# Spreading the score groups over the first three columns of a gated attention and MoE kernel

## The chip, the cores and the metric

The kernel runs on one core of a Trainium2 chip. The metric is the device time of one execution, in microseconds. The engines are named as in the profile: PE (TensorE, matmuls; PEld is its weight load), DVE (VectorE), ACT (ScalarE), POOL (GpSimd) and SP (SyncE, which here only starts transfers). Each engine works through its own list of instructions in order and waits on semaphores for the others.

## What is computed

```python
def _attn_ref(u, v, z):                     # u, v: 8 x 3008 x 256, z: 8 x 3008 x 64
    scale = 1.0 / S
    scores = scale * np.matmul(z, z.transpose(0, 2, 1))
    attn = np.maximum(scores, 0.0) ** 2
    out = np.matmul(attn, v)
    return (u * out).astype(np.float32)

def _moe_ref(x, w_in, w_out):               # x: 24064 x 256, w_in: 256 x 2048
    h = x @ w_in
    g = h * np.cos(h)
    return (g @ w_out).astype(np.float32)
```

The output of the first, flattened to 24064 rows, is the input of the second.

## The kernel before, in words

**Columns and pieces.** A batch has 3008 positions: 24 blocks of 128 (the last is a half), or 6 columns of 512. For each column J the kernel makes the squared ReLU of the scores against all blocks, in pieces A of four blocks by one column, key (b, J, I) with I from 0 to 5. A *score group* (emit_score, L178) makes half a piece: two matmuls (L187) of 64 rows each, which run side by side in the two halves of the array, into a two-bank score buffer E; a ReLU from PSUM into an r tile, on ACT (L200) or, for the groups listed in on_dve (8, 15, 21, 28, 34), on DVE (L198); and a square on DVE into the piece (L204 or L207). The score matrix is symmetric, so from column 3 of the first batch on a piece that exists already is turned by a DMA transpose on SP (L234, or L228 inside a diagonal piece) in place of being computed again. Columns 0 to 2 of the first batch, which this case is about, compute all of their 12 groups. The list of groups is fixed; done_groups counts through it.

**Value matmuls.** emit_value (L248) multiplies one block of a piece with v. For each block k and each half dh of the 256 output columns there are two such matmuls, t = 0 and 1, again side by side in the two halves of the array; below, such two are a *pair*. The four sums of a column are in the banks M0, M1 (dh = 0) and in one E buffer (dh = 1). A column has 23 blocks by 2 halves, and the last half block split over both halves: 47 pairs.

**Buffers.** PSUM holds M0, M1 and three score buffers E0, E1, E2 of two banks. take_e hands out E buffers in turn (e_order). In the first three columns one E buffer holds the dh = 1 sums, so the score groups have two. There are three r tiles and 22 pieces.

**Start.** z of the first batch comes in six pieces of four blocks. DVE casts pieces 0 and 1, POOL casts 2 to 5 (L501), between which it issues the first v loads. PE turns each piece (turn_on_pe, L505: four transposes of 128 x 128) into PSUM, and ACT or DVE copies it to zT (copy_turned, L513 and L515). Pieces 2 to 5 are turned into one tile, turned4, that lies where E2 will be; each turn into it waits for the copy of the one before. Matmuls on a zero tile (filler, L534) stand between them.

**Columns 0 to 2** (phase_a_first, L334). For each I, the four dh = 0 pairs and then the four dh = 1 pairs of piece I are issued, then a burst of quota[I] score groups, then a transpose or other small work. Four groups are made ahead of column 0; each later group belongs to a piece that is read about two I later, and the last four of each column to the next column. In column 0, the turns and copies of pieces 4 and 5 (last_pieces) stand between the first four dh = 0 pairs and the first dh = 1 pairs, since the dh = 1 sums go to E2. At the end of a column, gate_sum adds the two banks of each half: a copy on ACT (L260), then an add on DVE (L261). The products with u (gate_mul, L276) come in the next column after I = 1, and uT, the turned u, comes by a DMA transpose (turn_u, L156). hold (L332) is a small copy on POOL that keeps the load of the next u behind the sums.

**Around them.** Between columns 1 and 2 stand four blocks of the hidden layer (emit_h: L385 matmuls, ACT cosine L393, DVE product L395), and w_out is loaded on POOL's queue ahead of them (L561). After column 2 the kernel goes into its steady form: phase_b (hidden layer and output matmuls, L385 and L407) and phase_a (a later column) by turns, to the end.

Of the kernel before, what the change touches and what calls it, by code (L numbers as in the profile page):

```python
# [14 lines left out]
def kernel(  # L15
# [74 lines left out]
    def drop_piece(key):  # L90
        i = pieces.pop(key)
        if pending.get(i):
            pending[i] = "dropped"
        else:
            free_pieces.append(i)
# [53 lines left out]
    def load_u(s):  # L149
        t = upool.tile([P, 4, D], FP16, name="u16")  # L150
        load_rows(t, u, s // NC, s % NC)
        u16s[s] = t

    def turn_u(s):
        t = upool.tile([P, 8, P], FP16, name="uT")
        nc.sync.dma_start_transpose(t, u16s.pop(s).rearrange("p j d -> p (j d)"))  # L156
        uTs[s] = t
# [17 lines left out]
    turn_slots = {}  # L175
    done_groups = [0]

    def emit_score(on_dve=False):  # L178
        b, J, I, h = groups[done_groups[0]]
        done_groups[0] += 1  # L180
        cut = I == J and not (b == 0 and J < 3)
        W = 2 * P if cut and h == 0 else width(J)
        zT = zTs[b]
        e = E[take_e()]
        for t in range(2):
            k = 4 * I + 2 * h + t
            nc.tensor.matmul(  # L187
                e[:, t, 0:W],
                zT[t * H:(t + 1) * H, k * P:(k + 1) * P],
                zT[t * H:(t + 1) * H, J * CW:J * CW + W],  # L190
                start=True,
                stop=True,
            )
        key = (b, J, I)
        a = new_piece(key) if h == 0 else piece(key)
        r = rpool.tile([P, 2, CW], FP16, name="r")
        if on_dve:
            nc.vector.tensor_scalar(r[:, :, 0:W], e[:, :, 0:W], 0.0, None, ALU.max)  # L198
        else:
            nc.scalar.activation(r[:, :, 0:W], e[:, :, 0:W], AF.Relu)  # L200
        if I > J:
            a4 = a.rearrange("p (k t j) -> p t k j", k=4, j=P)[:, 2 * h:2 * h + 2, :, :]
            r4 = r.rearrange("p t (k j) -> p t k j", j=P)
            nc.vector.tensor_tensor(a4, r4, r4, ALU.mult)  # L204
        else:
            a4 = a.rearrange("p (k w) -> p k w", w=CW)[:, 2 * h:2 * h + 2, 0:W]
            nc.vector.tensor_tensor(a4, r[:, :, 0:W], r[:, :, 0:W], ALU.mult)  # L207
        if h == 0:
            return
        if cut or (I > J and (b, J, I) not in direct):  # L210
            turns.append(((b, I), key))
            turns.sort(key=lambda t: t[0])
            turn_slots[key] = pieces[key]
            pending[pieces[key]] = "held"

    def emit_turns(due, more=0):
        while turns and (turns[0][0] <= due or more > 0):
            if turns[0][0] > due:
                more -= 1
            (b, c), key = turns.pop(0)  # L220
            b, J, I = key
            i = turn_slots[key]
            a = piece_bufs[i]
            if I == J:
                a4 = a.rearrange("p (k w) -> p k w", w=CW)
                for rr in range(2, 4):
                    rows = P if J * 4 + rr < NB - 1 else H
                    nc.sync.dma_start_transpose(  # L228
                        a4[:, 0:2, rr * P:rr * P + rows],
                        a[0:rows, rr * CW:rr * CW + 2 * P],  # L230
                    )
            else:
                d = new_piece((b, I, J))
                nc.sync.dma_start_transpose(d.rearrange("p (n j) -> p n j", j=P), a)  # L234
            if pending.pop(i) == "dropped":
                free_pieces.append(i)
# [10 lines left out]
    def emit_value(b, J, k, t, dh, bank, start, stop):  # L247
        nc.tensor.matmul(  # L248
            bank[:, 0:width(J)],
            vs[b, k // 4][t * H:(t + 1) * H, k % 4, dh * P:(dh + 1) * P],  # L250
            value_rhs(b, J, k, t),
            start=start,
            stop=stop,
        )

    def gate_sum(s, b0, b1):
        W = width(s % NC)
        s0 = spool.tile([P, CW], FP32, name="s0")
        s1 = spool.tile([P, CW], FP32, name="s1")
        nc.scalar.copy(s0[:, 0:W], b0[:, 0:W])  # L260
        nc.vector.tensor_tensor(s1[:, 0:W], b1[:, 0:W], s0[:, 0:W], ALU.add)  # L261
        return s1

    def gate_mul(s, dh, s1):
        J = s % NC
        b = s // NC
        W = width(J)
        if s not in xs:
            if J == NC - 1 and b % 2 == 1:
                xs[s] = xodd  # L270
            else:
                xs[s] = xpool.tile([P, 2, CW], FP16, name="x")
        x = xs[s]
        uT = uTs[s].rearrange("p (k d) j -> p k d j", d=2)
        nk = W // P
        nc.vector.tensor_tensor(  # L276
            x[:, dh, 0:nk * P].rearrange("p (k j) -> p k j", j=P),
            s1[:, 0:nk * P].rearrange("p (k j) -> p k j", j=P),
            uT[:, 0:nk, dh, :],
            ALU.mult,  # L280
        )
        if nk < 4:
            dst = x[:, dh, nk * P:W] if b % 2 == 1 else xodd[:, dh, W:CW]
            nc.vector.tensor_tensor(
                dst, s1[:, nk * P:W], uT[:, nk, dh, 0:W - nk * P], ALU.mult
            )
# [44 lines left out]
    def hold(src):  # L331
        nc.gpsimd.tensor_copy(mark[:, 0:1], src)  # L332

    def phase_a_first(s, on_dve, quota, before_dh1=None):  # L334
        b, J = s // NC, s % NC
        if before_dh1 is None:
            ea = e_order.pop(0)
            acc = [M, [E[ea][:, 0, :], E[ea][:, 1, :]]]
        else:
            acc = [M, None]  # L340
        last = NB - 1
        for I in range(NC):
            for dh in range(2):
                if acc[dh] is None:
                    before_dh1()
                    ea = e_order.pop()
                    acc[1] = [E[ea][:, 0, :], E[ea][:, 1, :]]
                for k in range(4 * I, min(4 * I + 4, last)):
                    for t in range(2):
                        emit_value(  # L350
                            b, J, k, t, dh, acc[dh][t], k == 0,
                            k == last - 1 and t != dh,
                        )
            if I == NC - 1:
                emit_value(b, J, last, 0, 0, acc[0][0], False, True)
                emit_value(b, J, last, 1, 1, acc[1][1], False, True)
            drop_piece((b, J, I))
            if I == NC - 1:
                if s == 0:
                    turn_u(0)  # L360
                late_sums.extend(gate_sum(s, *acc[dh]) for dh in range(2))
                hold(late_sums[0][0:1, 0:1])
                load_u(s + 1)
            for _ in range(quota[I]):
                emit_score(on_dve=done_groups[0] in on_dve)
            if s > 0:
                emit_turns((0, 0), 1)
                if I == 0:
                    turn_u(s)
                if I == 1:  # L370
                    for dh in range(2):
                        gate_mul(s - 1, dh, late_sums.pop(0))
        e_order.append(ea)

    def mwidth(m):
# [134 lines left out]
    def copy_turned(g):  # L510
        dst = zTs[0][:, g * CW:(g + 1) * CW]
        if g == 0:
            nc.scalar.copy(dst, turned[g])  # L513
        else:
            nc.vector.tensor_copy(dst, turned[g])  # L515
# [16 lines left out]
    def filler(n):  # L532
        for i in range(n):
            nc.tensor.matmul(M[i % 2], warm[:, 0:P], warm, start=True, stop=True)  # L534

    on_dve = (8, 15, 21, 28, 34)
    emit_score()
    emit_score()
    filler(2)
    for g in range(2, 4):  # L540
        turn_on_pe(g)
        copy_turned(g)
        filler(1)
        emit_score()

    def last_pieces():
        for g in range(4, NC):
            turn_on_pe(g)
            copy_turned(g)
        E.append(ppool.tile([P, 2, CW], FP32, name="E2", tag="E2"))  # L550
        e_order.append(2)

    for g in range(2, NC):
        load_v(0, g)
    load_u(0)
    nc.gpsimd.dma_start(w_in16, moe_w_in.rearrange("(k p) f -> p k f", p=P))

    halves = [(0, NB // 2), (NB // 2, NB)]
    phase_a_first(0, on_dve, (2, 2, 2, 2, 2, 2), last_pieces)
    phase_a_first(1, on_dve, (3, 3, 2, 2, 2, 0))  # L560
    nc.gpsimd.dma_start(w_out16, moe_w_out.rearrange("(k p) f -> p k f", p=P))  # L561
    for i in range(4):
        emit_h(0, i)
    phase_a_first(2, on_dve, (3, 3, 3, 3, 2, 0))
    assert done_groups[0] == need[3]
    for dh in range(2):
        gate_mul(2, dh, late_sums.pop(0))
# [59 lines left out]
```

## Time and profile before

| | us |
|---|---|
| median of 9 runs | 1241.62 |
| lowest and highest | 1240.0, 1243.92 |
| the profiled execution | 1243.92 |
| its span in the profile | 1242.1 |
| PE busy | 1223.0 |
| DVE busy | 810.1 |
| ACT busy | 806.1 |

The profile shows one execution. A busy share of an engine is the time in which an instruction of it was under way; a matmul's end is modelled. A window row gives its start and end, its length, then busy time and (instructions) of PE, PEld, DVE, ACT and POOL, then the granted share of PE's full clock, the mean busy share of the DMA engines, and GB/s. A row of the chain gives start, duration, engine, written tile, line and count. "issue" in the chain is time in which the engine waited for nothing that the profile shows.

The first instructions of the start, from the timeline (start, duration, engine, line, what; in brackets the idle time before and what ended it):

```profile
4.91 0.60 POOL L501 CAST z<-z 128x512 f16<-128x512 f32 x1 [3.60 <-DMA z<-in_z_dram]
5.07 0.60 PE L187 MATMUL E<-zT 64*128 64x512 f16 x4 [0.29 <-ACT zT L513]
5.50 2.86 ACT L200 ACTIVATE r<-E 128x1024 f16<-128x1024 f32 x3 [0.49 <-PE E L187]
6.56 2.36 DVE L207 TENSOR_TENSOR A<-r 128x1024 f16<-128x1024 f16 x2 [1.31 <-ACT r L200]
7.67 1.72 POOL L501 CAST z<-z 128x512 f16<-128x512 f32 x2
8.85 0.41 DVE L515 COPY zT<-turned 128x512 f16<-128x512 f16 x1
9.31 0.38 PE L505 MATMUL turned<-id,z 128*128 128x128 f16 x4 [2.33 <-DVE zT L515]
10.07 1.31 PE L248 MATMUL M<-A,v 64*128 64x512 f16 x8
12.43 0.58 PE L505 MATMUL turned<-id,z 128*128 128x128 f16 x4 [0.52 <-DVE zT L515]
13.53 1.04 PE L248 MATMUL E<-A,v 64*128 64x512 f16 x4 [0.52 <-DVE zT L515]
```

The copy of piece 2 stands in DVE's list behind the first two squares (6.56 to 8.92), and the turn of piece 3 on PE waits for it.

### The profile page before, as it was taken

Reading aid. Unit: us, or ns where it says so; the run is one execution under the profiler, and the core shown is the slowest. Engines: PE = TensorE matmul, PEld = TensorE weight load, DVE = VectorE, ACT = ScalarE, POOL = GpSimd, SP = SyncE. Lnnn points to the kernel's source line nnn. Section 1 sums busy time; section 2 is a strip of 40 time slices with the busy share of each in tenths; the row PEclk is TensorE's granted clock in tenths of the full one; section 3 lists DMA queues with packets and bytes.
Section 4 is the critical chain, followed back from the end, with each engine's and each line's share of the span. In section 5 each row is a group of like instructions: output and inputs, shape, how many; then the busy total and the mean of one; then the engine's idle time right before and its main releaser. Section 6 shows DMA issues by size and latency. Waiting matters only on the chain.

```text
span 1242.1 us, 23270 instructions
## 1 busy us (share of the span) xinstructions
PE 1223.0 (98%) x9775; PEld 696.0 (56%) x9775; DVE 810.1 (65%) x947; ACT 806.1 (65%) x918; POOL 132.2 (11%) x185
## 2 busy tenths in 40 slices
PE   8799999999999999999999999999999999999998
PEld 3355655556555555555555555655555555555565
DVE  5866766666666666666666666666666666666555
ACT  5666667666666666666666676666766666666445
POOL 3030211003000030000300003000121001000000
PEclk8999999999999999999999999999999999999999
DMA  9999797649976499844998359972597726953201
GB/s 144 157 159 157 100 173 130 118 90 120 149 118 120 81 117 160 139 87 98 143 143 134 69 98 153 163 120 69 104 173 125 133 60 110 162 102 69 46 18 51
DMA packets 467161, 144.80 MB, mean 117 GB/s; under 512 B 391536, under 2 KB 466800, under 8 KB 467056
## 3 DMA queue, kind: packets, MB, share of 16 engines
q1 hardware_dynamic: 368304, 110.11, 50.1%
q0 software_dynamic: 97216, 32.78, 26.9%
q8 instruction: 76, 1.25, 0.4%
q10 hardware_dynamic: 1536, 0.43, 0.2%
q14 instruction: 29, 0.24, 0.1%
HBM read 66.32 MB, written 24.64 MB: 73 GB/s over the span
## 4 chain that ended last, share of the span: by engine, by line
PE 96%; DVE 2%; ACT 1%; issue 1%; ACTq 0%; DVEq 0%
PE M L407 26%; PE E L385 26%; PE M L248 20%; PE E L248 19%; PE E L187 5%; ACT r L200 1%; DVE g L395 0%; DVE r L198 0%; DVE A L207 0%; DVE s L261 0%; PE E L520 0%; ACT c L393 0%; DVE A L204 0%; PE E L407 0%; DVE zT L515 0%
## 5 line engine op out<-in xcount | busy, mean ns | idle before, releaser
L395 DVE SCALAR_TENSOR_TENSOR g<-E,c 128x1024 f16<-128x1024 f32 (+1 forms) x384 | 456.7, 1201 | 219.7 <-ACT c L393 218.4
L393 ACT ACTIVATE c<-E 128x1024 f16<-128x1024 f32 (+1 forms) x384 | 381.1, 1006 | 182.0 <-PE E L385 181.6
L200 ACT ACTIVATE r<-E 128x1024 f16<-128x1024 f32 (+1 forms) x337 | 323.5, 965 | 132.1 <-PE E L187 125.2
L407 PE MATMUL M<-w_out,g 128*128 128x256 f16 x2992 | 373.7, 273 | 1.1 <-DVE g L395 0.6
L248 PEld LDWEIGHTS <-v 64*128 64x128 f16 x4512 | 218.7, 94 | 262.9 <-issue 24.9
L385 PE MATMUL E<-x,w_in 128*128 128x512 f16 (+1 forms) x1408 | 347.6, 375 | 0.6 <-DVE s L261 0.3
L407 PEld LDWEIGHTS <-g 128*128 128x128 f16 x3008 | 294.2, 98 | 94.0 <-DVE g L395 0.9
L248 PE MATMUL M<-A,v 64*128 64x512 f16 (+1 forms) x2256 | 282.8, 374 | 0.6 <-DVE s L261 0.5
L248 PE MATMUL E<-A,v 64*128 64x512 f16 (+1 forms) x2256 | 277.0, 373 | 0.5 <-DVE zT L515 0.5
L204 DVE TENSOR_TENSOR A<-r 128x1024 f16<-128x1024 f16 x240 | 165.5, 692 | 109.6 <-ACT r L200 108.5
L385 PEld LDWEIGHTS <-w_in 128*128 128x128 f16 x1536 | 146.4, 98 | 126.3 <-issue 21.0
L187 PE MATMUL E<-zT 64*128 64x512 f16 (+2 forms) x684 | 123.5, 363 | 8.4 <-DVE r L198 4.1
L426 ACT ACTIVATE o<-M 128x512 f32<-128x512 f32 x94 | 50.2, 585 | 63.4 <-PE M L407 63.4
L207 DVE TENSOR_TENSOR A<-r 128x512 f16<-128x512 f16 (+1 forms) x102 | 58.7, 577 | 46.5 <-ACT r L200 45.5
L136 POOL DMA_DIRECT2D u<-in_u_dram x48 | 36.8, 771 | 454.8 <-DMA uT<-u 454.4
L136 POOL DMA_DIRECT2D v<-in_v_dram x48 | 35.9, 754 | 403.9 <-PE E L187 341.0
L187 PEld LDWEIGHTS <-zT 64*128 64x128 f16 x684 | 34.7, 94 | 51.0 <-issue 13.1
L276 DVE TENSOR_TENSOR x<-s,uT 128x512 f16<-128x512 f32 (+1 forms) x88 | 59.5, 679 | 2.8
L261 DVE TENSOR_TENSOR s<-E,s 128x512 f32<-128x512 f32 (+1 forms) x48 | 32.6, 680 | 34.8 <-ACT s L260 34.8
L260 ACT COPY s<-E 128x512 f32<-128x512 f32 (+1 forms) x48 | 27.8, 579 | 39.7 <-PE E L248 39.7
L261 DVE TENSOR_TENSOR s<-M,s 128x512 f32<-128x512 f32 (+1 forms) x48 | 32.4, 675 | 6.0 <-ACT s L260 6.0
L260 ACT COPY s<-M 128x512 f32<-128x512 f32 (+1 forms) x48 | 27.5, 573 | 8.2 <-PE M L248 7.8
(33 smaller groups left out, 125.4 us busy)
## 6 DMA issues: line engine op xcount, KB each, us to landing
out_dram<-o SPq DMA_DIRECT2D x87, 256.0 KB, 2.7
v<-in_v_dram POOLq DMA_DIRECT2D x40, 256.0 KB, 6.7
u<-in_u_dram POOLq DMA_DIRECT2D x40, 256.0 KB, 9.4
z<-in_z_dram POOLq DMA_DIRECT2D x14, 368.0 KB, 15.6
A<-A SPq DMA_TRANSPOSE x207, 4.4
v<-in_v_dram POOLq DMA_DIRECT2D x8, 192.0 KB, 11.1
u<-in_u_dram POOLq DMA_DIRECT2D x8, 192.0 KB, 4.1
out_dram<-o SPq DMA_DIRECT2D x10, 128.0 KB, 2.8
```

The costliest lines, as they stand in the source:

```text
L136: nc.gpsimd.dma_start(t[:, 0:full, :], src[b, g * CW:g * CW + full * P, :].rearrange("(j p) d -> p j d", p=P),)
L187: nc.tensor.matmul(e[:, t, 0:W], zT[t * H:(t + 1) * H, k * P:(k + 1) * P], zT[t * H:(t + 1) * H, J * CW:J * CW + W], start=True, stop=True,)
L200: nc.scalar.activation(r[:, :, 0:W], e[:, :, 0:W], AF.Relu)
L204: nc.vector.tensor_tensor(a4, r4, r4, ALU.mult)
L207: nc.vector.tensor_tensor(a4, r[:, :, 0:W], r[:, :, 0:W], ALU.mult)
L248: nc.tensor.matmul(bank[:, 0:width(J)], vs[b, k // 4][t * H:(t + 1) * H, k % 4, dh * P:(dh + 1) * P], value_rhs(b, J, k, t), start=start, ...
L261: nc.vector.tensor_tensor(s1[:, 0:W], b1[:, 0:W], s0[:, 0:W], ALU.add)
L276: nc.vector.tensor_tensor(x[:, dh, 0:nk * P].rearrange("p (k j) -> p k j", j=P), s1[:, 0:nk * P].rearrange("p (k j) -> p k j", j=P), uT[:, ...
L385: nc.tensor.matmul(e[:, f, 0:W], w_in16[:, k, ft * P:(ft + 1) * P], x[:, k, 0:W], start=(k == 0), stop=(k == 1),)
L393: nc.scalar.activation(c[:, :, 0:W], e[:, :, 0:W], AF.Sin, bias=half_pi, scale=inv_s2)
L395: nc.vector.scalar_tensor_tensor(g[:, :, 0:W], e[:, :, 0:W], 1.0, c[:, :, 0:W], ALU.mult, ALU.mult)
L407: nc.tensor.matmul(y_bank(m, k), gs[m, ft // 2][:, ft % 2, k * P:(k + 1) * P], w_out16[:, ft, :], start=(ft == 0 and (k % 2 == 0 or (final ...
```

## The change

In the columns, the steps of a column (47 pairs) are listed first, and n score groups are placed singly after given steps: with n = 12 after steps 2, 5, 9, 12, 16, 20, 23, 27, 31, 34, 38, 42, with n = 14 after 2, 5, 8, 11, 14, 17, 20, 23, 26, 29, 32, 35, 38, 42. The number of groups a column, their order and the on_dve list are as before. The sums of a column now follow its last pair with no score group in between. A piece is dropped, a transpose and turn_u or the gate multiplies are issued, right after the last pair of an I.

At the start, piece 2 is turned and copied ahead of the first score group. A square can be held back (later), and the squares of the first four groups are put behind copies: DVE's list is now copy 2, copy 3, square 0, square 1, copy 4, square 2, copy 5, square 3. All six pieces are turned before the first value matmul, two of the four filler matmuls are gone, and column 0 takes its E2 buffer at its beginning like the other columns. The lists on POOL and SP keep their order.

```diff
-    def emit_score(on_dve=False):
+    def emit_score(on_dve=False, later=None):
...
+        def square():
+            if I > J:
+                a4 = a.rearrange("p (k t j) -> p t k j", k=4, j=P)[:, 2 * h:2 * h + 2, :, :]
+                r4 = r.rearrange("p t (k j) -> p t k j", j=P)
+                nc.vector.tensor_tensor(a4, r4, r4, ALU.mult)
...
+        if later is None:
+            square()
         else:
-            a4 = a.rearrange("p (k w) -> p k w", w=CW)[:, 2 * h:2 * h + 2, 0:W]
-            nc.vector.tensor_tensor(a4, r[:, :, 0:W], r[:, :, 0:W], ALU.mult)
+            later.append(square)
...
-    def phase_a_first(s, on_dve, quota, before_dh1=None):
+    def phase_a_first(s, n):
         b, J = s // NC, s % NC
...
+        ea = e_order.pop(0)
+        acc = [M, [E[ea][:, 0, :], E[ea][:, 1, :]]]
         last = NB - 1
...
+        steps = [
+            (dh, k)
+            for I in range(NC)
+            for dh in range(2)
+            for k in range(4 * I, min(4 * I + 4, last))
+        ] + [(2, last)]
+        lo, hi = 2, 42
+        at = {}
+        for i in range(n):
+            p = lo + (hi - lo) * i // (n - 1)
+            at[p] = at.get(p, 0) + 1
+        for i, (dh, k) in enumerate(steps):
+            if dh == 2:
                 emit_value(b, J, last, 0, 0, acc[0][0], False, True)
                 emit_value(b, J, last, 1, 1, acc[1][1], False, True)
...
+            else:
+                for t in range(2):
+                    emit_value(
+                        b, J, k, t, dh, acc[dh][t], k == 0, k == last - 1 and t != dh
+                    )
+            if dh > 0 and (k % 4 == 3):
+                drop_piece((b, J, k // 4))
+                if s > 0:
+                    emit_turns((0, 0), 1)
+                    if k < 4:
+                        turn_u(s)
+                    elif k < 8:
+                        for d in range(2):
+                            gate_mul(s - 1, d, late_sums.pop(0))
+            for _ in range(at.get(i, 0)):
                 emit_score(on_dve=done_groups[0] in on_dve)
...
+        if s == 0:
+            turn_u(0)
+        late_sums.extend(gate_sum(s, *acc[dh]) for dh in range(2))
+        hold(late_sums[0][0:1, 0:1])
+        load_u(s + 1)
         e_order.append(ea)
...
+    squares = []
+    turn_on_pe(2)
+    copy_turned(2)
+    emit_score(later=squares)
+    emit_score(later=squares)
+    turn_on_pe(3)
+    filler(1)
+    copy_turned(3)
+    squares.pop(0)()
+    emit_score(later=squares)
+    squares.pop(0)()
+    turn_on_pe(4)
+    filler(1)
+    copy_turned(4)
+    emit_score(later=squares)
+    squares.pop(0)()
+    turn_on_pe(5)
+    copy_turned(5)
+    squares.pop(0)()
+    E.append(ppool.tile([P, 2, CW], FP32, name="E2", tag="E2"))
+    e_order.insert(0, 2)
...
-    phase_a_first(0, on_dve, (2, 2, 2, 2, 2, 2), last_pieces)
-    phase_a_first(1, on_dve, (3, 3, 2, 2, 2, 0))
+    phase_a_first(0, 12)
+    phase_a_first(1, 12)
...
-    phase_a_first(2, on_dve, (3, 3, 3, 3, 2, 0))
+    phase_a_first(2, 14)
```

More of the change, by code (lines that the diff above doesn't have):

```diff
@@ L200, in emit_score @@
             nc.scalar.activation(r[:, :, 0:W], e[:, :, 0:W], AF.Relu)
[L201 to L204, printed above, removed]
-        else:
-            a4 = a.rearrange("p (k w) -> p k w", w=CW)[:, 2 * h:2 * h + 2, 0:W]
-            nc.vector.tensor_tensor(a4, r[:, :, 0:W], r[:, :, 0:W], ALU.mult)
+        def square():
[4 more added lines that the diff above has]
+            else:
+                a4 = a.rearrange("p (k w) -> p k w", w=CW)[:, 2 * h:2 * h + 2, 0:W]
+                nc.vector.tensor_tensor(a4, r[:, :, 0:W], r[:, :, 0:W], ALU.mult)
+        if later is None:
+            square()
+        else:
+            later.append(square)
         if h == 0:
@@ L332, in hold @@
         nc.gpsimd.tensor_copy(mark[:, 0:1], src)
-    def phase_a_first(s, on_dve, quota, before_dh1=None):
+    def phase_a_first(s, n):
         b, J = s // NC, s % NC
[L336 to L340, printed above, removed]
-        last = NB - 1
[L342 to L354, printed above, removed]
+        ea = e_order.pop(0)
+        acc = [M, [E[ea][:, 0, :], E[ea][:, 1, :]]]
+        last = NB - 1
+        steps = [
[11 more added lines that the diff above has]
+            if dh == 2:
@@ L355, in phase_a_first @@
                 emit_value(b, J, last, 0, 0, acc[0][0], False, True)
                 emit_value(b, J, last, 1, 1, acc[1][1], False, True)
[L357 to L364, printed above, removed]
-                emit_score(on_dve=done_groups[0] in on_dve)
@@ L366, in phase_a_first @@
[L366 to L372, printed above, removed]
+            else:
+                for t in range(2):
[11 more added lines that the diff above has]
+                            gate_mul(s - 1, d, late_sums.pop(0))
@@ L536 @@
     on_dve = (8, 15, 21, 28, 34)
[L537 to L551, printed above, removed]
+    squares = []
[19 more added lines that the diff above has]
+    e_order.insert(0, 2)
     for g in range(2, NC):
```

## The prediction

> **What bounds the kernel now.** I read the page first, for where TensorE is not full:
>
> ```profile
> span 1242.1 us, 23270 instructions
> ...
> PE   8799999999999999999999999999999999999998
> ...
> PEclk8999999999999999999999999999999999999999
> ...
> PE 96%; DVE 2%; ACT 1%; issue 1%; ACTq 0%; DVEq 0%
> ```
>
> TensorE is the bound (96% of the chain that ended last), and only the first two or three of the 40 slices have room. Then the windows, cut at the stages: start, column 0, column 1, the four blocks of hidden layer (emit_h), column 2, first output stage, rest.
>
> ```profile
> core 0: us, PE busy (x) PEld busy (x) DVE busy (x) ACT busy (x) POOL busy (x), PEclk, DMA share, GB/s
> 0.00:10.07 10.07, 6.26 (x36) 2.52 (x37) 5.02 (x9) 5.04 (x6) 5.86 (x13) 1.00 0.72 113
> 10.07:28.40 18.33, 17.13 (x129) 7.96 (x126) 9.55 (x15) 10.44 (x12) 4.81 (x8) 0.81 1.21 182
> 28.40:45.50 17.10, 13.79 (x118) 6.33 (x116) 13.45 (x20) 11.55 (x13) 0.96 (x2) 1.00 0.65 114
> 45.50:50.00 4.50, 3.94 (x20) 1.50 (x20) 4.27 (x6) 4.15 (x6) 2.07 (x3) 1.00 1.03 162
> 50.00:70.90 20.90, 15.70 (x124) 7.08 (x124) 14.18 (x20) 12.04 (x13) 0.00 (x0) 0.92 1.07 157
> 85.50:1242.00 1156.50, 1151.98 (x9263) 661.26 (x9262) 753.25 (x870) 753.71 (x860) 109.74 (x148) 1.00 0.75 114
> ```
>
> After 85.5 us TensorE idles 4.5 us in 1156, so whatever column 2 gains is carried to the end. In the columns the clock is granted at 0.81 and 0.92, and busy time (which contains modelled ends) falls short of the span. Last the chain in order of time, in column 2:
>
> ```profile
> 55.67 0.23 PE E L187 x2
> ...
> 56.84 1.94 ACT r L200 x2
> ...
> 59.41 1.29 DVE x L276 x2
> 60.70 1.15 DVE r L198
> ...
> 62.29 1.71 PE M L248 x8
> 64.00 1.57 PE E L248 x8
> ```
>
> A burst of three score groups has two score buffers; the third waits for a ReLU (ACT L200, or DVE L198 behind two gate multiplies L276). The value matmuls after it then stand at 1.71 us for eight, where the chain elsewhere has 0.86: half clock.
>
> **The price of one step.** Eight value matmuls are four pairs: 0.86 / 4 = 0.215 us a pair. Four score matmuls are two groups in 0.43: 0.215 a group. A column is 47 pairs. With 12 groups it is 59 x 0.215 = 12.7 us, with 14 it is 61 x 0.215 = 13.1. Before, columns 0 to 2 and the hidden blocks took 60.8 us (10.07 to 70.9).
>
> **The score's latency,** from the timeline: group at t, ReLU 0.43 later (5.07 to 5.50), 1.02 long, square 0.03 later, 0.69 long: the square ends at t + 2.2. Queued ReLUs follow 0.92 apart (two in 1.94), queued squares 0.61. In the new order groups are 4 or 5 steps apart (3 or 4 pairs and themselves): 0.86 to 1.08 us. With two buffers a group may start when the ReLU two before it is over, t + 1.5 against 1.7 to 2.2: no wait on ACT. A DVE ReLU (1.22) is another matter, below. Pieces are due late enough: groups 4 and 5 stand at steps 2 and 5, their piece is read at step 16, 11 pairs and 3 groups or 3.0 us later, against 2.2.
>
> **Start.** Piece 2's cast ends at 5.51 (POOL 4.91 + 0.60); its turn now precedes the first score group, which slips from 5.07 to about 5.8. DVE copies pieces 2 and 3 by about 7.75 (cast 3 ends 6.99, four turns, copy 0.42). Then squares 0 and 1: 2.36 us for two beside POOL's casts, less where those are over (9.39): done about 9.8. Copy 4 ends 10.2, piece 5 is turned by 10.5, and the first value matmul stands at 10.5 (10.07 before). The v piece it needs was there at 10.07; the second, issued at 6.92 with a median landing of 5.5, is there at 12.4, its first use at 10.5 + 8 pairs + 2 groups = 12.65. Square 2 and copy 5 end at 11.3, so the fifth pair, into E2, stands at 11.6, where it stood at 13.53. If the squares take 1.2 us to the end, all of this is 0.7 later.
>
> **Column 0.** 12.7 us, plus the DVE ReLU of group 8: square 7 ends 1.12 after group 8 starts, the ReLU at 2.34; group 10, which needs the buffer, is due after 9 steps, 1.94. Wait 0.45. Ends at 10.5 + 13.15 = 23.65.
>
> **Column 0 to 1.** Before, two groups stood behind the sums as cover. Now none does, and group 15 (DVE ReLU) stands at step 42. From its start: square 14 ends at 1.12, ReLU 2.34, square 15 at 3.0, the sum that frees bank M1 at 3.7 (add 0.68). The column ends at 5 steps, 1.08. TensorE waits 2.6 us; before, 0.5 with work in front. Next at 26.25.
>
> **Column 1.** 12.7, plus group 21: its ReLU is queued behind two gate multiplies (1.29) and square 20. From group 20: square 19 ends at 1.1, multiplies 2.35, square 20 at 3.0, ReLU 4.25; group 23 is due after 14 steps, 3.0. Wait 1.25. Ends at 40.2.
>
> **Hidden blocks.** Unchanged, bound by DVE: 45.54 to 49.98, 4.45 us. To 44.65.
>
> **Column 2.** 13.1, plus 1.1 for its first groups, which wait for DVE to empty E0 and E1 (0.32 + 0.74 before; the groups come earlier now, so there is no less), plus group 34 behind the multiplies. From group 32: square 32 ends at 2.2, multiplies 3.45, square 33 at 4.1, ReLU 5.35; group 36 is due after 16 steps, 3.45. Wait 1.9. Ends at 60.75. The handover to the output stage is as before.
>
> **Transfers.** The order on SP and POOL is the same; w_out is issued after column 1's sums. Its 14.9 us from 48.17 end 15.9 after that sum (46.46 + 0.68 = 47.14); in the new walk the sum ends near 41.6, w_out lands at 57.5, and is read near 61.9. Cover 4.4 us. u, turned beside it in 10.3, ends no later.
>
> **Sum.** 70.9 - 60.75 = 10.1 us gained, half clock not counted. For that:
>
> ```profile
> 7.27:10.68 3.41, 1.37 (x13) 0.69 (x14) 3.00 (x5) 1.50 (x3) 3.41 (x5) 1.00 1.10 123
> 31.16:34.57 3.41, 2.05 (x18) 0.99 (x19) 2.29 (x4) 2.52 (x3) 0.00 (x0) 1.00 0.57 71
> 58.47:61.88 3.41, 1.07 (x10) 0.43 (x7) 3.15 (x6) 1.33 (x2) 0.00 (x0) 1.00 1.76 173
> 61.88:65.30 3.42, 3.41 (x18) 1.54 (x19) 1.62 (x3) 0.60 (x1) 0.00 (x0) 0.50 0.96 211
> ```
>
> The clock fell after stretches of 3.41 us in which TensorE was busy 40% and 31%, and did not after one of 60%. A full stretch at half clock costs 1.7. In the new walk three stretches can come near 40%: the start, the 2.6 us wait, the 1.9 us wait; it hangs on how the stretches lie. Bounds: no fall, 0; three, 5.1. I take 1.0, nearer the first, since each wait fills a stretch only if it lies wholly inside.
>
> [...]
>
> Gain 9.1. The profiled execution took 1243.92, its span 1242.1 and 1.8 around it: 1243.92 - 9.1 = **1234.8**. It is the longest of the nine runs, 2.3 over their median; as its two clock falls (3.4) are already taken out, I subtract no more.
>
> **Rivals.**
> - *Waits and clock take half back (0.12).* All three waits drop the clock: 1234.8 + 4.1 = 1238.9. For: DVE is already the fullest of the small engines (13.45 of 17.1 in column 1). Against: full columns restore the clock in one stretch.
> - *Start only (0.05).* Even spacing gives nothing because the DVE ReLUs set the pace: 20.9 and 17.1 stay, column 0 ends at 26.25 with its wait in place of 29.14 (M1's restart): 1243.92 - 2.9 = 1241. For: waits of 1.25 and 1.9 remain. Against: of the waits before score groups, 3.6 us in four are on ACT, in the third group of a burst, and there are no bursts left.
> - *w_out becomes the bound (0.06): slower.* The stage shrinks by 10 us but the transfer doesn't; transposes share it. TensorE waits at the first output matmul once w_out lands after 61.9, and the kernel is slower once it lands after 61.9 + 9.1 = 71, 28.6 us from issue, where 14.9 was seen. At 30 us: 1245.3. Against: twice the measured time.
>
> **How the numbers follow.** Forecast 0.77, its own range 1231.5 (no fall, and the 2.3 to the median taken off) to 1237.5 (a second and third fall in part). To 1239 with the first rival. About 0.2% (2.5 us) can be told from no change: faster is below 1239.1, forecast and nearly all of the first rival, 0.88; same 0.06; slower 0.06.
>
> **What would show it.** Right: first E2 value matmul near 11.6; score groups alone between pairs; waits before L187 only behind DVE ReLUs; a bare wait of 2.6 at column 0's end; column 2 ending near 61 to 62. Wrong: ReLU waits at every group, half clock over a whole column, or PE waiting for w_out.

## The result, and the profile after

| | before | changed |
|---|---|---|
| median, us | 1240.8 (32 runs) | 1235.34 (10 runs) |
| lowest and highest | 1239.8, 1243.92 | 1233.56, 1238.14 |
| the profiled execution | 1243.92 | 1235.34 |
| its span | 1242.1 | 1233.6 |

The ratio of the changed kernel to the one before is 0.9955, 95% interval 0.9948 to 0.9963: 5.5 us less by the medians (8.5 between the two profiled spans; why the two differ is shown below). The median of before is that of all 32 runs, 0.8 under the nine known at the prediction.

The windows of the changed kernel, cut at the same stages as those of before (start, column 0, column 1, the four hidden blocks, column 2, and the rest after the first output stage):

```profile
core 0: us, PE busy (x) PEld busy (x) DVE busy (x) ACT busy (x) POOL busy (x), PEclk, DMA share, GB/s
0.00:10.44 10.44, 7.76 (x41) 3.41 (x42) 5.01 (x10) 5.95 (x7) 6.36 (x14) 1.00 0.71 112
10.44:23.75 13.31, 13.26 (x120) 6.11 (x119) 9.98 (x16) 9.91 (x10) 4.24 (x7) 1.00 1.19 179
23.75:41.70 17.95, 15.02 (x118) 7.15 (x117) 12.64 (x18) 11.82 (x13) 0.96 (x2) 0.90 0.93 160
41.70:46.16 4.46, 3.91 (x18) 1.47 (x17) 4.12 (x5) 4.14 (x6) 2.07 (x3) 1.00 1.08 190
46.16:62.40 16.24, 13.92 (x124) 6.89 (x124) 14.22 (x20) 11.92 (x13) 0.00 (x0) 1.00 1.30 189
77.10:1233.40 1156.30, 1151.79 (x9262) 661.19 (x9258) 753.25 (x870) 753.55 (x860) 110.82 (x150) 1.00 0.76 115
```

Column 0 went from 18.33 us to 13.31 and column 2 from 20.90 to 16.24. Column 1, with the wait before it, stands at 17.95: its clock is 0.90, and the wait at column 0's end (23.75 to 26.11) lies in it. The rest takes 1156.30 us against 1156.50: what the columns gained was carried to the end.

What TensorE waited for from 10 us to the end of column 2 (what waited and for what: us in total, times, longest):

```profile
PE E L187 <- DVE r L198: 2.6, 2, 1.6
PE M L254 <- DVE s L267: 1.3, 1, 1.3
PE turned L513 <- DVE zT L523: 1.0, 1, 1.0
PE M L254 <- ACT s L266: 0.7, 1, 0.7
```

Before, the first lines of the same view (10 to 72 us) were:

```profile
PE E L187 <- DVE r L198: 4.1, 4, 2.3
PE E L187 <- ACT r L200: 3.6, 4, 0.9
```

The waits on ACT's ReLUs are gone; two waits on DVE's are left. What stands in front of them on DVE, in column 2 of the changed kernel (timeline; L205 square, L282 gate multiply, L198 ReLU):

```profile
53.05 0.69 DVE L205 TENSOR_TENSOR A<-r 128x1024 f16<-128x1024 f16 x1 [0.22 <-ACT r L200]
53.66 1.29 DVE L282 TENSOR_TENSOR x<-s,uT 128x512 f16<-128x512 f32 x2
54.86 0.68 DVE L205 TENSOR_TENSOR A<-r 128x1024 f16<-128x1024 f16 x1
55.46 1.22 DVE L198 TENSOR_SCALAR r<-E 128x1024 f16<-128x1024 f32 x1
```

And TensorE at the same place and at column 0's end:

```profile
54.26 0.83 PE L254 MATMUL M<-A,v 64*128 64x512 f16 x6
56.73 0.28 PE L187 MATMUL E<-zT 64*128 64x256 f16 x2 [1.65 <-DVE r L198]
```

```profile
23.35 0.38 PE L254 MATMUL M<-A,v 64*128 64x512 f16 x1
23.37 0.38 PE L254 MATMUL E<-A,v 64*128 64x512 f16 x1
24.40 0.37 PE L254 MATMUL M<-A,v 64*128 64x512 f16 x1 [0.65 <-ACT s L266]
26.11 0.80 PE L254 MATMUL M<-A,v 64*128 64x512 f16 x5 [1.33 <-DVE s L267]
26.55 0.57 PE L187 MATMUL E<-zT 64*128 64x512 f16 x2
26.77 0.57 PE L254 MATMUL M<-A,v 64*128 64x512 f16 x2
26.99 1.21 PE L254 MATMUL E<-A,v 64*128 64x512 f16 x4
```

One score group fell due at 54.9 (three pairs after 54.26) and ran at 56.73, when DVE's ReLU (55.46 + 1.22) was over. At column 0's end TensorE has one matmul between 23.6 and 26.11, and soon after that the four E matmuls take 1.21 us where 0.6 is usual: the clock has fallen, granted at 0.50 from 27.21 to 30.63 us.

### The profile page after: what moved, and what is told of

Read it like the earlier page. It is cut to its first block, busy times and chain, and to the rows that moved or that the text cites. A ratio compares the mean times of both kernels' runs of the same rounds, so it can differ in the third digit from the quotient of the medians.

```text
span 1233.6 us, 23267 instructions
## 1 busy us (share of the span) xinstructions
PE 1220.0 (99%) x9773; PEld 695.6 (56%) x9773; DVE 809.5 (66%) x947; ACT 806.6 (65%) x918; POOL 132.1 (11%) x185
## 3 DMA queue, kind: packets, MB, share of 16 engines
q8 instruction: 76, 1.25, 0.4%
## 4 chain that ended last, share of the span: by engine, by line
PE 96%; DVE 2%; ACT 1%; issue 1%; DMA 0%; POOL 0%; SPq 0%; ACTq 0%
PE M L415 26%; PE E L393 26%; PE M L254 19%; PE E L254 18%; PE E L187 5%; ACT r L200 1%; DVE g L403 0%; DVE r L198 0%; DVE A L208 0%; DMA z<-in_z_dram 0%; DVE s L267 0%; DVE A L205 0%; DVE x L282 0%; ACT c L401 0%; PE E L415 0%
## 5 line engine op out<-in xcount | busy, mean ns | idle before, releaser
L205 DVE TENSOR_TENSOR A<-r 128x1024 f16<-128x1024 f16 x240 | 165.4, 691 | 104.8 <-ACT r L200 103.8
L187 PE MATMUL E<-zT 64*128 64x512 f16 (+2 forms) x684 | 127.5, 364 | 3.5 <-DVE r L198 2.6
L282 DVE TENSOR_TENSOR x<-s,uT 128x512 f16<-128x512 f32 (+1 forms) x88 | 59.5, 679 | 2.8
## 6 DMA issues: line engine op xcount, KB each, us to landing
z<-in_z_dram POOLq DMA_DIRECT2D x14, 368.0 KB, 15.6
```

Of the source, the lines that this page charges most:

```text
L187: nc.tensor.matmul(e[:, t, 0:W], zT[t * H:(t + 1) * H, k * P:(k + 1) * P], zT[t * H:(t + 1) * H, J * CW:J * CW + W], start=True, stop=True,)
L282: nc.vector.tensor_tensor(x[:, dh, 0:nk * P].rearrange("p (k j) -> p k j", j=P), s1[:, 0:nk * P].rearrange("p (k j) -> p k j", j=P), uT[:, ...
```

## The experiments

Each ratio compares a run with runs of before on the same chip. The experiments ran in three sets, each on a chip of its own; the medians of before were 1241.47 (the two parts alone, none on DVE, 8 and 28 on DVE), 1240.25 (the two with zero-tile matmuls, the kernel before with none on DVE, u ahead) and 1241.46 (the new start with none on DVE, u further back). Where medians of different sets are subtracted below, the difference by the ratios stands beside it.

### The two parts alone

The new start with the old bursts (against the changed kernel; phase_a_first itself is that of before):

```diff
...
-    phase_a_first(0, 12)
+    phase_a_first(0, on_dve, (2, 2, 2, 2, 2, 2))
-    phase_a_first(1, 12)
+    phase_a_first(1, on_dve, (3, 3, 2, 2, 2, 0))
-    phase_a_first(2, 14)
+    phase_a_first(2, on_dve, (3, 3, 3, 3, 2, 0))
```

> The new start (turns and copies ahead of the squares) with the old bursts of two and three groups. Theory (the two parts gain separately): the first E2 pair moves from 13.53 to about 11.5, 1.9 to 2.5 us, and columns 1 and 2 keep their waits: 1238 to 1239, against 1240.8 before. Rival (the start's gain is lost again in the burst waits of column 0, since the groups behind it do not come earlier): 1240 to 1241.

Measured: 1238.63, ratio 0.9984 (0.9975 to 0.9993). The first E2 pair stands at 11.25 in place of 13.53, as expected, and the waits on ReLUs are those of before (4.1 and 3.6 us in the same view).

Even spacing with the old start (against the kernel before; phase_a_first is that of the changed kernel, with last_pieces put in when the first dh = 1 pair comes):

```diff
...
-    phase_a_first(0, on_dve, (2, 2, 2, 2, 2, 2), last_pieces)
+    phase_a_first(0, 12, last_pieces)
```

> The even spacing with the old start (pieces 4 and 5 turned inside column 0). Theory: the waits of columns 1 and 2 shrink as in the changed kernel (column 1 from 17.1 us to about 15, column 2 from 20.9 to about 16), the first E2 pair stays near 13.5: 1236.5 to 1238. If the parts add up, the gains of this run and of the start alone sum to the 5.5 us between the medians. Rival (most of the gain is the start's and its clock): 1239 or more.

Measured: 1239.39, ratio 0.9981 (0.9973 to 0.9990). A miss by 1.4 us, and inside the rival's range; but the start alone did not bring most of the gain, as that rival would have it. Its runs lie in two groups, five at 1238.0 to 1238.1 with a granted clock of 0.998 to 0.999, and six at 1239.4 to 1239.7 with 0.997 to 0.998; the median and the profile are of the second. By the ratios the two parts alone give 0.16% and 0.19%, 0.35% together, where both in one kernel gave 0.45% (0.37 to 0.52): some 1.2 us seem to be missing. In its profile value matmuls stand at half pace in two places: four take 0.86 us from 14.99 to 15.85 and from 32.12 to 32.98, where 0.43 is usual. TensorE in the 3.41 us before each slow place (3.41 us is also what the half clock of the changed kernel lasted, 27.21 to 30.63), and before a place where the pace stayed (six in 0.64 from 62.62):

```profile
10.75:14.16 3.41, 1.21 (x15) 0.69 (x12) 2.14 (x4) 1.18 (x2) 3.41 (x6) 1.00 1.02 130
27.82:31.23 3.41, 1.44 (x11) 0.65 (x12) 2.85 (x4) 1.07 (x2) 0.95 (x2) 1.00 0.18 40
58.53:61.94 3.41, 1.77 (x18) 0.88 (x16) 3.38 (x5) 1.62 (x2) 0.00 (x0) 1.00 1.75 152
```

Before the two slow places it was busy 35% and 42%, in the third line 52%. The first holds the old start's waits for the copies of pieces 4 and 5 (1.7 and 0.5 us), the second the new bare wait at column 0's end.

### The clock by itself

Eight matmuls on the zero tile are put in the bare wait. They compute nothing that is used.

```diff
         load_u(s + 1)
+        if s == 0:
+            for i in range(8):
+                nc.tensor.matmul(
+                    E[e_order[0]][:, i % 2, :], warm[:, 0:P], warm, start=True, stop=True
+                )
```

> The changed kernel with eight matmuls on a zero tile (1.7 us) into a free score buffer in the 2.6 us wait at column 0's end; they compute nothing that is used. Theory (the clock falls after a stretch of 3.41 us in which TensorE is busy under about half, 44% or less here and 50% or more where it stayed): no fall follows column 0, and the median drops by the price of a fall, 1.7 us, to 1233.6, the lowest run of the changed kernel. Rival (the fall has another cause, or the extra matmuls delay what follows): 1235 to 1236, with the fall still near 27.

Measured: 1234.15 (1233.64 to 1239.15, 6 runs), ratio 0.9954 (0.9941 to 0.9967). The profiled execution (1234.22) has no fall: its granted clock is 1.000, and four E matmuls from 27.54 take 0.79 us, against 1.21 in the changed kernel; M1's restart is no earlier (26.66 us; its column 0 also waited 0.8 us for a load of v). The granted clock is 1.000 in five of its six runs, and in one of the eleven of the changed kernel on record. The median is 1.2 below the changed kernel's 1235.34, but with one run at 1239.15 and another set of runs of before the two ratios show no difference. That the fall goes is seen directly; its price in the median is not settled by this run.

The same in the spread with the old start, and zero-tile matmuls in its two other waits as well:

```diff
     for g in range(2, 4):
+        if g == 3:
+            filler(8)
         turn_on_pe(g)
...
         for g in range(4, NC):
+            if g == 5:
+                for i in range(7):
+                    nc.tensor.matmul(
+                        E[e_order[0]][:, i % 2, :], warm[:, 0:P], warm, start=True, stop=True
+                    )
             turn_on_pe(g)
```

> Even spacing with the old start, with zero-tile matmuls in its three waits (eight ahead of piece 3's turn, seven ahead of piece 5's, eight at column 0's end). Theory (with the falls taken off, the two parts add: the old start costs 2.0 us of waiting and, in most executions, a fall): both falls of the profile of the spread alone (14.2 and 31.2) are gone and the median drops by up to 3.4 us, to 1236 to 1237. Rival (the parts interact through the groups' order, not the clock): 1238.5 to 1239.5.

Measured: 1236.44, ratio 0.9966 (0.9955 to 0.9978), and no fall in its profile (granted clock 1.000). That is 2.95 below the same kernel without them (1239.39, other set), or 0.15% by the ratios, 1.9 us. With the falls gone from both profiles, the old start costs 1236.44 - 1234.15 = 2.3 us more than the new (same chip); in the two profiles M1 starts again after column 0 at 29.15 and at 26.66, 2.5 us apart. So the clock can account for what was missing in the sum of the parts. That anything was missing is not certain: the intervals of the ratios also allow the two parts to add up.

### What makes the waits that are left

No ReLU on DVE, and then only two of the five:

```diff
-    on_dve = (8, 15, 21, 28, 34)
+    on_dve = ()
```

> The changed kernel with no ReLU on DVE. Theory: the waits that are left in the columns are made by ReLUs that queue on DVE behind squares and gate multiplies (1.9 to 2.6 us at column 0's end, 1.25 in column 1, 1.9 in column 2); without them about 1.4 us is left at column 0's end and nothing at the other two: 4 us less, 1231 to 1232. Rival (the five ReLUs relieve ACT, and without them ACT sets the pace at 0.92 us a group plus the sums' copies): TensorE waits for ACT at most groups of column 2, 1235 to 1238.

```diff
-    on_dve = (8, 15, 21, 28, 34)
+    on_dve = (8, 28)
```

> The changed kernel with groups 8 and 28 alone on DVE; 15, 21 and 34 go to ACT. Theory: these three make nearly all of the waits (0.8 + 1.25 + 1.9 us): 1231 to 1232, within 0.7 of the run with none on DVE. Rival (any DVE ReLU costs its wait alike): half way, 1233 to 1234.

Measured: 1230.40, ratio 0.9911 (0.9898 to 0.9925), and 1231.32, ratio 0.9918 (0.9905 to 0.9932). Both are some 4 to 5 us under the changed kernel (0.44% and 0.37% by the ratios), with one line; the two are not told apart by their intervals. TensorE's waits with none on DVE, in the same view as above:

```profile
PE turned L513 <- DVE zT L523: 1.0, 1, 1.0
PE M L254 <- ACT s L266: 0.7, 1, 0.7
PE E L187 <- DVE g L403: 0.5, 1, 0.5
PE M L254 <- DVE s L267: 0.5, 1, 0.5
```

No score group waits for a ReLU any more, ACT's neither: at the new spacing ACT keeps up alone. The wait for M1 went from 1.3 to 0.5. No fall is left in either profile (granted clock 1.000 in both).

The same line in the kernel before, with its bursts:

> The kernel before, bursts and all, with no ReLU on DVE. Theory (with bursts of three on two buffers the third group waits for a ReLU whatever engine makes it): a wait of about 0.9 takes the place of each DVE wait, except the one of 2.35 behind the gate multiplies, and the gain is 1 to 3 us: 1238 to 1240. Rival (the DVE ReLUs were the whole trouble, and the spacing would not have been needed): 1234 or less.

Measured: 1236.78, ratio 0.9972 (0.9964 to 0.9980). Better than expected by over 1 us. TensorE's waits (9 to 72 us) are as expected:

```profile
PE E L187 <- ACT r L200: 4.9, 6, 0.9
PE turned L505 <- DVE zT L515: 3.0, 2, 2.0
```

Six waits on ACT, none over 0.9 us, took the place of 4.1 + 3.6. What I had left out is the clock: its profile shows no half pace in columns 0 to 2 (eight value matmuls take 0.86 to 0.96 us there; in the kernel before they take 1.71 after the wait of 2.35), and the granted clock is 1.000 in ten of its twelve runs. The profiled execution is the slowest of them (1241.85, 5.1 above the median); what held it up lies in column 3 and comes below.

The new start with bursts and no ReLU on DVE:

> New start, old bursts, no ReLU on DVE. Theory (start and spacing are separate terms whatever makes the ReLUs): 2.0 us under the old start with no ReLU on DVE (1236.8), 1234.5 to 1235; the spacing is then worth 4 us more, down to 1230.4. Rival (with the ReLUs on ACT the bursts cost little, and the start does the rest): 1232.5 or less.

Measured: 1234.77, ratio 0.9948 (0.9934 to 0.9961). So, with no ReLU on DVE, the start is worth 1236.78 - 1234.77 = 2.0 us (0.24% by the ratios, 3.0 us) and the spacing 1234.77 - 1230.40 = 4.4 (0.37%, 4.6 us). Taking the ReLUs from DVE is worth 3.5 us in the kernel before (1240.25 to 1236.78, 0.28%) and 4.9 in the changed one (0.44%); the intervals do not tell these two apart.

### What is late next

The run with groups 8 and 28 on DVE has a profiled execution of 1232.76 whose columns end only 0.6 us later than those of the run with none. The other 2.4 us lie in column 3: TensorE waits 2.1 us there for the sums' add on DVE, which stands behind this (waits between 58 and 100 us):

```profile
DVE x L282 <- DMA uT<-u: 7.0, 1, 7.0
```

The gate multiply of column 3 waits for the transpose of u. On SP's queue that transpose stands behind two transposes of pieces that column 3 does not read. Two experiments move it, both with no ReLU on DVE. Ahead of them:

```diff
                 if s > 0:
-                    emit_turns((0, 0), 1)
+                    if s < 2 or k < 12:
+                        emit_turns((0, 0), 1)
```

> No ReLU on DVE, and the last three transposes of column 2 that no work waits for yet are put behind the transpose of u for column 3. In the run with 8 and 28 on DVE TensorE waited 2.1 us in column 3 for that u (DVE 7.0 us), and in the run with none on DVE DVE waited 4.4. Theory (the transpose queue is what is late next): uT lands 4 us or more earlier, DVE doesn't wait for it, and the time is that of the run with none on DVE without its slower executions: 1229.5 to 1230.2. Rival (the transfers together are the limit, and another one is late in its place): 1230.5 or more.

Measured: 1230.23 (1229.46 to 1233.98, 6 runs), ratio 0.9922 (0.9910 to 0.9934). In its profile DVE doesn't wait for uT at all (the multiply runs at 78.54 in place of 83.01), but the median is that of the run with none on DVE within both ranges. One run of 1233.98 was not profiled; what held it up is open.

And one transpose further back:

```diff
-    emit_turns((0, 3))
+    emit_turns((0, 3), 1)
     turn_u(3)
```

> Evenly spaced, no ReLU on DVE, and the transpose of u for column 3 put one transpose further back (three in front of it that no work waits for, where there were two). Theory (TensorE waits in column 3's sums for this transpose when it lands after about 84): uT lands 3 to 5 us later than 82.9, TensorE waits 2 to 4 us before the hidden layer's matmuls in column 3, 1232.5 to 1234. Rival (DVE's wait for it is covered and does not reach TensorE): 1230 to 1231.

Measured: 1232.37 (1231.42 to 1235.02, 5 runs), ratio 0.9934 (0.9921 to 0.9946). Its profiled execution is the fastest of the five, and there already:

```profile
PE E L393 <- DVE s L267: 1.6, 1, 1.6
```

```profile
DVE x L282 <- DMA uT<-u: 6.5, 1, 6.5
```

With none on DVE DVE waited 4.4 us and TensorE not at all; at 6.5 it waits 1.6, at 7.0 it waits 2.1. So in these two about 4.9 us of DVE's wait were covered by column 3's matmuls, and the rest was TensorE's. The slow profiled execution of the kernel before with no ReLU on DVE is a third case (waits between 58 and 110 us):

```profile
DVE x L276 <- DMA uT<-u: 8.0, 1, 8.0
PE E L385 <- DVE s L261: 3.2, 1, 3.2
```

There 4.8 us were covered. The granted clock of that execution is 0.999, which a run of 1236.83 also has. The wait of 3.2 us and, as an estimate, one fall (1.7 us, half of the 3.42 us at 0.50 from 61.88 in the profile of before) would be 4.9 of the 5.1 us by which that execution is above its median.

The best versions are those evenly spaced with no ReLU on DVE, with or without the earlier transpose (1230.23 and 1230.40, not told apart): both beat the kernel before and the changed one.

## Why the prediction was right

The time was 1235.34 against 1234.8, inside the range.

| step | predicted, us | profile |
|---|---|---|
| first value matmul | 10.5 | 10.44 |
| first E2 pair | 11.6 | 11.53 |
| column 0: wait for group 8's ReLU | 0.45 | about 0.2 |
| M1 free again after column 0 | 26.25 | 26.11 |
| column 1: wait behind the gate multiplies | 1.25 | 1.3 |
| column 1 ends | 40.2, with no fall | 41.7 |
| hidden blocks | 4.45 | 4.46 |
| column 2: wait behind the gate multiplies | 1.9 | 1.8 |
| column 2 ends | 60.75, with no fall | 62.3 |

The waits behind DVE in this table are counted from when the group fell due, at 0.215 us a step; the bracket in the timeline counts from the modelled end of the last matmul (0.94 in column 1, where the group fell due at 35.14 and ran at 36.45).

**Pace and start.** One price of 0.215 us for a pair or a group, and one chain ReLU, square for the pieces, were enough for both; that the old waits on ACT go and DVE's stay is seen in the waits. Column 0 also waited about 0.2 us for a load of v (at 14.96), which the sum did not have.

**DVE's ReLUs.** The sums gave 0.45 + 2.6 + 1.25 + 1.9 us of new or left waits. I named DVE's ReLUs as their cause and still took them as the price of the spacing. Taking the ReLUs away showed that all of it is theirs but 1.2 us at column 0's end (0.7 + 0.5), and that DVE was not needed for them: 4.9 us, with the fall that goes along.

**The clock.** I took 1.0 us, a little over half a fall. One fall came, after the bare wait at column 0's end (0.50 from 27.21 to 30.63 us), at a price of about 1.6: column 1 took 15.6 us from 26.11, against 13.95. So the stage gained 70.9 - 62.3 = 8.6 us against 9.1; that term was small by about 0.6 us. The granted clock differs between runs of one kernel (0.997 to 1.000 in the eleven of the changed kernel), so the prediction could not know how many falls would come: that the time came so near 1234.8 is in part luck, though one fall more or less would have left it in the range too.

**The base.** The sum was made against the profiled execution of before, which was the slowest of the runs known; that was right for the time (1243.92 - 1235.34 = 8.6), and too large by 3 us for the gain between medians. That execution has two falls (0.50 from 10.68 and from 61.88 us). Of the 32 runs of before, 16 lie within 1239.8 to 1240.2, 11 within 1241.4 to 1241.8, four near 1242.8 and one at 1243.92: the medians of the first two groups stand 1.7 us apart (1241.68 and 1240.01), about the price of one fall. The granted clock on record for the 47 runs of before beside the experiments goes with the groups: 0.999 to 1.000 up to 1240.25, 0.998 to 0.999 from 1241.3 to 1241.8, 0.997 near 1242.8, and 0.996 in the profiled execution, where 3.41 us at half clock are 0.0014 of the mean (1.7 of 1242.1 us). So the falls are the likely cause of the groups; that they are the only one is not shown.

**Transfers.** w_out was issued at 44.36 and landed in 12.2, at 56.6, ahead of its use at 63.2, as worked out. What my check of the transfers left out is the transpose of u for column 3. It did not show in this kernel's profile, but it cost TensorE 1.6 to 3.2 us in three profiles of kernels with fewer or no ReLUs on DVE.

**The rivals.** Waits and clock taking half back: one fall in place of three. Start only: the start alone gave 0.16% of the 0.45%, so no. w_out as the bound: covered by 6.6 us.

## What to carry to other kernels

Where two engines share one kind of work to balance their loads, look at what stands ahead of each in its list: five ReLUs on DVE stood behind squares and gate multiplies and cost 4.9 us (a clock fall among it), though no engine but TensorE was full. An average load does not tell it; the wait list of the stage does. And take a base for a sum from an execution whose clock falls are counted, because a wait that a change removes may be worth more than its length: here the bare wait at column 0's end went with a fall that cost about 1.6 us more.

## What the runs showed of the hardware

These are readings from the profiles of this case. In the profile of before the granted clock stands at 0.50 from 10.68 to 17.51 us and from 61.88 to 65.30, in that of the changed kernel from 27.21 to 30.63. In the 3.41 us before these three TensorE was busy 40%, 31% and 43%, and its longest single wait there was 2.33, 2.35 and 1.33 us. In the spread alone half pace followed 35% and 42%, in the start alone 36% (1.23 of 3.42 us before 57.78; eight value matmuls from 58.11 then take 1.70 us, where 0.86 is usual). Counted on from the falls of before and of the changed kernel through the first 130 us, in steps of 3.41, the least busy stretches after which the clock stayed at 1.00 have 60% (before, 31.16 to 34.57) and 52% (changed, 54.52 to 57.93); in the spread alone 7.34 to 10.75 has 50%, and the row after it stands at 1.00. What lies between 43% and 50% was not shown. The stretch of the changed kernel before its fall, the next, and the one in column 2 that no fall followed:

```profile
23.80:27.21 3.41, 1.48 (x13) 0.68 (x14) 2.82 (x4) 1.04 (x2) 0.96 (x2) 1.00 1.22 214
27.21:30.63 3.42, 3.42 (x20) 1.51 (x18) 1.38 (x2) 2.05 (x2) 0.00 (x0) 0.50 0.99 131
54.52:57.93 3.41, 1.76 (x19) 0.85 (x17) 3.38 (x6) 1.59 (x3) 0.00 (x0) 1.00 1.42 137
```

In these two profiles the clock was back at 1.00 after 3.41 us in which TensorE was busy all the time (before from 14.09 and from 61.88, after from 27.21), and still at 0.50 after a stretch of 70% (before, 2.38 us busy from 10.68 to 14.09). In the profile of before the two falls, at 10.68 and 61.88, are 51.20 us apart, 15 times 3.41. The fall at 10.68 and the one at 27.21 in the changed kernel are 16.53 us apart, 4.84 times 3.41: counted from the start of the span, such steps lie differently in these two executions.
